# An order planned in the source for the second stage of an S4 and SwiGLU kernel, with the first kernel block's spectra kept in DRAM

## The chip, the cores and the metric

The kernel runs on one core of one Trainium2 chip. The metric is device time in microseconds from the start to the end of one execution; "before" is a median of three runs. A core has a matrix engine (TensorE, PE in the profile), two engines for elementwise work (VectorE, DVE, and ScalarE, ACT), a general engine (GpSimd, POOL) and a queue for transfers (SyncE, SP). Each engine works through its own instructions in the order in which the program lists them, and waits on semaphores for the others.

## What is computed

Two layers, each an S4 long convolution with a residual and then a SwiGLU feed-forward with a residual, over 2048 tokens of width 512 (F = 1376):

```python
def _A_ref(u, ...):                       # L = 2048, D = 512, N = 128
    P = jnp.exp(logdA[:, :, None] * l[None, None, :])
    K = jnp.einsum("dn,dnl,dn->dl", Cc, P, dB).real
    Kf, Uf = rfft(pad(K)), rfft(pad(u))   # length 2 L
    return irfft(Uf * Kf)[:L] + u * Dskip

def _B_ref(x, w_gate, w_up, w_down):
    return (silu(x @ w_gate) * (x @ w_up)) @ w_down

x = A_u
x = x + _A_ref(_layernorm(x), ...)
x = x + _B_ref(_layernorm(x), ...)
x = x + _A_ref(_layernorm(x), ...)
x = x + _B_ref(_layernorm(x), ...)
```

## The kernel before

The sequence is cut into four blocks of 512 tokens. The convolution is done by blocks in the frequency domain: a block's input has a spectrum u (eight pieces of 256 KB: two halves h of the width, four residues q), the convolution kernel has four blocks of spectra w, and output block b is the sum over k = 0..b of w[k] times u[b - k].

The first stage (to about 325 us) makes the kernel's spectra and the first two input spectra; its order is written out by hand in `tc.manual_schedule`, which fixes the order of ScalarE, VectorE and TensorE. Spectra of kernel blocks 1 to 3 go to DRAM (`wdr`); those of block 0 stay in SBUF in `w0r` (16 KB in each partition).

The second stage goes through the eight pairs of layer and block in the order of `SEQ`: (0,0), (0,1), (0,2), (1,0), (0,3), (1,1), (1,2), (1,3). The text calls them blocks 0 to 7 in this order. For each there are:

- `inputs` and `forward` (lines 245 to 279, 680 to 707), from block 2 on: load, layernorm on ScalarE, folding on VectorE (tiles bt and z), 12 matmuls into `pf`, copy to u, and a store to `udr` by a POOL queue for later blocks.
- `ssm` (from line 709): for each of the eight pieces b + 1 complex products, each one multiplication of VectorE over 128x1024 (line 755) and, from the second on, one addition (line 758); joining (759, 760), splitting into two halves of 16 bits (763 on ScalarE, line 232 on VectorE), 12 matmuls into `pi` (774), combining, and per half h two groups of six and eight operations that add to the residual in `xs` (lines 788 to 808).
- `ffn_norm` (line 812), per half s of 256 tokens: layernorm and four transposing transfers issued by SP (line 840).
- `ffn` (line 870), per half s: a `remainder` of 96 columns (lines 852 to 854, its result transposed by four transfers), five groups of 48 matmuls into `pgu` (lines 885 to 887; the tag has two PSUM buffers, which `py` and the remainder share), each evacuated by silu (890, ScalarE), product (891, VectorE), high half (892, ScalarE), low half (893, VectorE); then the down product `py` in two rows r of 128 tokens, 33 matmuls each (lines 899 to 901), each followed by an addition of VectorE (line 904) and a store.

The weights come as 32-bit values and are split into two 16-bit halves each, `his` on ScalarE and `los` on VectorE (lines 641, 646, 667, 670), in 19 parts. The first few are done in the hand-written stage, and so are the rest, after the first norm: one high and one low part in turn, with a `fetch` now and then, behind the last outputs of block 0.

From there the order is the framework's. It schedules all engines by the program's order as priority, with raised priority for evacuations, norms, pi and pf (`tc.high_priority`), and a timeline model of its own. The program lists the convolution of block i + 1 ahead of the feed-forward of block i:

```python
    for i, lb in enumerate(SEQ):
        if i + 1 < len(SEQ):
            take(itertools.chain(*ssm(*SEQ[i + 1])), 100)
        ffn(*lb, ready if i == 0 else None)
```

Of the kernel before, what the change touches and what calls it, by code (L numbers as in the profile page):

```python
# [22 lines left out]
P = 128  # L23
# [18 lines left out]
HALF = 2  # L42
INV = 1
# [38 lines left out]
def kernel(ctx, tc, x, a_re, a_im, b_re, b_im, c_re, c_im, log_dt, d_skip,  # L82
# [10 lines left out]
                xf=1, nn=1, hh=1, hl=1, sg=2, hf=1, stats=2, stats2=2, ef=1)  # L93
# [38 lines left out]
    w0r = sb.tile([P, 2, 4, 2, HD], F32, name="w0r")  # L132
# [106 lines left out]

    def norm_x(n):  # L240
        rs, nb = row_stats(n, 4, 1.0, "stats", lambda r: tl([P, D], "junk", "t1", BF16))
        for c in range(4):
            A.activation(n[:, c], n[:, c], AF.Identity, scale=rs[:, c:c + 1], bias=nb[:, c:c + 1])

    def forward(n, h, eh):


        hs = slice(h * HD, (h + 1) * HD)
        x0, x1, x2, x3 = (n[:, c, hs] for c in range(4))
        bt = tl([P, 7, HD], "bt", "bt")  # L250
        a_, b_, p_, q_, r_, s_, hx = (bt[:, i] for i in range(7))
        stt(a_, x2, HH, x0, OP.add)
        stt(b_, x2, -HH, x0, OP.add)
        A.activation(hx, x2, AF.Copy, scale=HH)
        stt(p_, x3, TT, x1, OP.add)
        stt(r_, x3, -TT, x1, OP.add)
        stt(q_, x1, TT, x3, OP.subtract)
        stt(s_, x1, TT, x3, OP.add)
        for i, q in enumerate(QORD):
            z = z2[:, 0 if eh else i % 2]  # L260
            u_, v_ = ((p_, a_) if q in (0, 3) else (q_, b_))
            stt(z[:, 0], u_, CC if q < 2 else -CC, v_, OP.add)
            stt(z[:, 1], s_ if q in (0, 3) else r_, CC, hx, OP.add if q < 2 else OP.subtract)
            if eh:
                hl = z2[:, 1].bitcast(F16).rearrange("p i (l d) -> p l i d", l=2)
                A.activation(hl[:, 0], z, AF.Copy, scale=256.0)
                stt(hl[:, 1], z, 256.0, hl[:, 0], OP.subtract)
            pf = psml([P, 2, HD], "pf")
            with tc.high_priority(offset=BOOST):
                for o in range(2):  # L270
                    if eh:
                        terms = [(eh[:, q, o + i, le], hl[:, lz, i]) for i in range(2) for le, lz in ((0, 0), (0, 1), (1, 0))]
                    else:
                        terms = [(ef[:, q, o + i], z[:, i]) for i in range(2)]
                    for k, (e, m) in enumerate(terms):
                        PE.matmul(pf[:, o], lhsT=e, rhs=m, start=k == 0, stop=k == len(terms) - 1)  # L276
                u = tl([P, 2, HD], "u", "u")
                A.activation(u, pf, AF.Copy, scale=2.0 ** -16 if eh else 1.0)  # L278
            yield q, u
# [400 lines left out]
    def inputs():  # L680

        for layer, b in SEQ:
# [160 lines left out]
    def remainder(pgu, nh, nlo, hh, hl):  # L843

        rows = TB // P
        fs = slice(F - FR, F)
        pr = pgu.rearrange("p a b t -> p (a b t)")[:, :rows * 2 * FR].rearrange("p (r w f) -> p r w f", r=rows, w=2)
        for r in range(rows):
            rc = slice(r * P, (r + 1) * P)
            for wi in range(2):  # L850
                for k in range(4):
                    PE.matmul(pr[:, r, wi], lhsT=nh[:, k, rc], rhs=wgu(wi, k, 0)[:, fs], start=k == 0, stop=False)
                    PE.matmul(pr[:, r, wi], lhsT=nh[:, k, rc], rhs=wgu(wi, k, 1)[:, fs], start=False, stop=False)
                    PE.matmul(pr[:, r, wi], lhsT=nlo[:, k, rc], rhs=wgu(wi, k, 0)[:, fs], start=False, stop=k == 3)
# [337 lines left out]
```

## Time and profile before

| | |
|---|---|
| median of three runs | 1191.55 us (1190.38 to 1193.35) |
| the profiled execution | 1191.82 us, its span 1190.0 us |
| TensorE busy | 1108.1 us, 93% |
| VectorE busy | 1026.7 us, 86% |
| ScalarE busy | 618.8 us, 52% |
| GpSimd busy | 178.9 us, 15% |
| moved by DMA | 146.91 MB, mean 123 GB/s |
| first feed-forward product (line 885) | at 329.3 us |

The page gives busy times, the span in slices, the chain of work that ended last, the costliest groups of instructions and the transfers. In a row of the order of time the columns are start, duration, engine, line, operation, output and inputs, and in brackets the idle time of the engine ahead of it and what ended it. The duration of a matmul is its whole way through the array; the next one starts before it ends, so the distance of two starts is what one costs.

### The profile page before, as it was taken

The page shows a single profiled execution, that of the slowest core. Times are in us where ns is not written, and L with a number is a line of the kernel's source. Part 1 is how long each engine was busy: PE and PEld are TensorE (multiplying, and loading weights), DVE is VectorE, ACT ScalarE, POOL GpSimd, SP SyncE. Part 2 cuts the span into 40 slices and gives each one's busy share as a digit, 9 for nine tenths or more (in the row PEclk, how much of TensorE's full clock was granted, in tenths as well). Part 3 has the DMA queues.
Part 4 walks back from the last instruction along what each step waited for, and adds up shares of the span by engine and source line. Part 5 has one row for each costly group of instructions (what it writes and reads, how often), then busy time and mean ns, then how long its engine had stood idle before and what let it go on. Part 6 is the DMA issues. An engine that isn't in the chain of part 4 may idle for free.

```text
span 1190.0 us, 25245 instructions
## 1 busy us (share of the span) xinstructions
PE 1108.1 (93%) x10268; PEld 859.4 (72%) x10268; DVE 1026.7 (86%) x1623; ACT 618.8 (52%) x1168; POOL 178.9 (15%) x233
## 2 busy tenths in 40 slices
PE   2979999889978998999999999999999999999998
PEld 2857766667866766777777686868677686877875
DVE  8989999996899989999999999998997899983211
ACT  6998788763255445357744263564533552334211
POOL 3105444432300011011010000210200010000000
PEclk9999999999979998999999999999999999999999
DMA  6454455568468326442334443432445144312000
GB/s 235 124 138 129 109 128 125 118 184 232 146 199 248 103 72 187 129 129 89 103 94 142 135 149 128 145 107 98 130 131 191 45 120 129 114 51 45 14 24 18
DMA packets 138471, 146.91 MB, mean 123 GB/s; under 512 B 77873, under 2 KB 87089, under 8 KB 138354
## 3 DMA queue, kind: packets, MB, share of 16 engines
q1 hardware_dynamic: 133490, 128.51, 35.7%
q0 software_dynamic: 4864, 16.78, 5.8%
q8 instruction: 80, 1.31, 0.5%
q14 instruction: 37, 0.30, 0.1%
HBM read 98.19 MB, written 28.31 MB: 106 GB/s over the span
## 4 chain that ended last, share of the span: by engine, by line
PE 48%; DVE 32%; ACT 9%; issue 6%; DMA 3%; POOL 1%; SPq 1%; DVEq 0%; ACTq 0%; POOLq 0%
PE pgu L885 8%; PE pgu L887 8%; PE pgu L886 8%; PE pi L774 4%; DVE t L755 4%; PE pw L552 3%; PE py L899 3%; PE py L900 3%; PE py L901 3%; PE pf L276 3%; DVE yk L758 2%; DVE z L232 2%; DVE yk L755 2%; DVE im L394 1%; DVE sg L891 1%
## 5 line engine op out<-in xcount | busy, mean ns | idle before, releaser
L885 PE MATMUL pgu<-mix,wsl 128*128 128x256 f16 x1280 | 352.2, 275 | 9.1 <-DVE sg L891 5.5
L886 PE MATMUL pgu<-mix,wsl 128*128 128x256 f16 x1280 | 352.1, 275 | 1.2 <-DVE mix L831 1.2
L887 PE MATMUL pgu<-mix,wsl 128*128 128x256 f16 x1280 | 351.9, 275 | 0.4 <-DVE wsl L646 0.4
L886 PEld LDWEIGHTS <-wsl 128*128 128x128 f16 x1280 | 126.1, 99 | 27.1 <-issue 10.5
L887 PEld LDWEIGHTS <-wsl 128*128 128x128 f16 x1280 | 126.1, 99 | 21.1 <-DVE wsl L646 3.6
L885 PEld LDWEIGHTS <-wsl 128*128 128x128 f16 x1280 | 126.1, 99 | 16.9
L899 PE MATMUL py<-wsl,hh 128*128 128x512 f16 (+1 forms) x352 | 133.6, 380 | 4.3 <-DVE xf L904 2.5
L901 PE MATMUL py<-wsl,hl 128*128 128x512 f16 (+1 forms) x352 | 133.5, 379 | 0.0
L900 PE MATMUL py<-wsl,hh 128*128 128x512 f16 x320 | 121.4, 379 | 0.0
L755 DVE TENSOR_TENSOR t<-uu,w 128x1024 f32<-128x1024 f32 x96 | 117.1, 1220 | 0.7 <-DMA uu<-udr 0.6
L758 DVE TENSOR_TENSOR yk<-yk,t 128x1024 f32<-128x1024 f32 x96 | 117.0, 1219 | 0.3
L890 ACT ACTIVATE sg<-pgu,sc 128x512 f32<-128x512 f32 x80 | 54.5, 682 | 104.2 <-PE pgu L887 97.6
L774 PE MATMUL pi<-yl,mix 128*128 128x256 f16 x672 | 92.3, 273 | 7.5 <-ACT yl L763 6.0
L552 PE MATMUL pw<-kt,ek 128*128 128x256 f32 (+2 forms) x420 | 98.5, 373 | 0.0
L891 DVE SCALAR_TENSOR_TENSOR sg<-pgu,sc,sg 128x512 f32<-128x512 f32 x80 | 59.7, 747 | 43.7 <-ACT sg L890 43.5
L892 ACT ACTIVATE hh<-sg 128x512 f16<-128x512 f32 x80 | 50.1, 626 | 76.6 <-DVE sg L891 76.5
L552 PEld LDWEIGHTS pw<-kt,ek 128*128 128x128 f32 x420 | 78.2, 195 | 9.7
L227 POOL TENSOR_TENSOR rs<-mv,mhalf 128x2 f32<-128x2 f32 (+1 forms) x21 | 39.3, 1870 | 255.1 <-ACT mv L226 240.6
L774 PEld LDWEIGHTS <-mix 128*128 128x128 f16 x672 | 65.3, 98 | 13.6 <-issue 1.8
L276 PE MATMUL pf<-z,eh 128*128 128x256 f16 x576 | 74.9, 275 | 0.0
L763 ACT ACTIVATE yl<-mix,sy 128x512 f16<-128x512 f32 x56 | 40.1, 717 | 63.4 <-DVE mix L760 63.3
L755 DVE TENSOR_TENSOR yk<-u,w0r 128x1024 f32<-128x1024 f32 x56 | 68.3, 1220 | 0.3 <-ACT u L278 0.3
(250 smaller groups left out, 2232.6 us busy)
## 6 DMA issues: line engine op xcount, KB each, us to landing
w<-wdr SPq DMA_DIRECT2D x96, 256.0 KB, 2.7
uu<-udr SPq DMA_DIRECT2D x96, 256.0 KB, 3.0
udr<-u POOLq DMA_DIRECT2D x32, 256.0 KB, 2.4
wdr<-wo SPq DMA_DIRECT2D x96, 64.0 KB, 2.3
udr<-u SPq DMA_DIRECT2D x16, 256.0 KB, 2.5
g<-tmp POOLq DMA_DIRECT2D x8, 512.0 KB, 4.7
g<-btl POOLq DMA_DIRECT2D x8, 512.0 KB, 6.1
n<-xdr SPq DMA_DIRECT2D x4, 1024.0 KB, 5.7
```

The source lines that it names most:

```text
L276: PE.matmul(pf[:, o], lhsT=e, rhs=m, start=k == 0, stop=k == len(terms) - 1)
L552: PE.matmul(pw[:, i], lhsT=e, rhs=kt[:, :, c + 4 * k0:4 * k1:4, :].rearrange("p g k d -> p k g d"), start=c == 0, stop=c == 3)
L755: V.tensor_tensor(t, uu.unsqueeze(1).to_broadcast([P, 2, 2, HD]), w.unsqueeze(2).to_broadcast([P, 2, 2, HD]), OP.mult)
L758: V.tensor_tensor(yk, yk, t, OP.add)
L774: PE.matmul(pi[:, o], lhsT=e, rhs=m, start=k == 0, stop=k == len(terms) - 1)
L885: PE.matmul(o, lhsT=wgu(wi, k, 0)[:, fs], rhs=nh[:, k], start=k == 0, stop=False)
L886: PE.matmul(o, lhsT=wgu(wi, k, 0)[:, fs], rhs=nlo[:, k], start=False, stop=False)
L887: PE.matmul(o, lhsT=wgu(wi, k, 1)[:, fs], rhs=nh[:, k], start=False, stop=k == 3)
L891: V.scalar_tensor_tensor(sg, pgu[:, 1], sc6[:, 4:5], sg, OP.mult, OP.mult)
L899: PE.matmul(py[:, r], lhsT=hh[:n, f, rc], rhs=wd(f, 0)[:n], start=f == 0, stop=False)
L900: PE.matmul(py[:, r], lhsT=hh[:n, f, rc], rhs=wd(f, 1)[:n], start=False, stop=False)
L901: PE.matmul(py[:, r], lhsT=hl[:n, f, rc], rhs=wd(f, 0)[:n], start=False, stop=f == FT - 1)
```

## The change

From the first feed-forward product on, the order of TensorE, VectorE, ScalarE and of the emission to SP and POOL is planned in the source. The program first builds a list of jobs (`plan_splits`, `plan_ssm`, `plan_forward`, `plan_norm`, `plan_ffn`), each with its engine, an estimated duration and latency, the jobs that it depends on, a priority, and buffers that it takes and gives back. `emit` then simulates the engines: it always takes the job that can start first, and among those that can start at the same time on an engine the one with the lowest priority tuple. The instructions are emitted in that order, inside `manual_schedule`.

- Priorities (lower first): evacuations (0, 0, ..), weight splits (0, 1, k), the last outputs of block 0 (0, 2), then the work of block i by (1, i, ..). On TensorE pi and pf have (0, i, ..) and count as ready 1500 ns after their inputs (`MARGIN`).
- The spectra of kernel block 0 are written from `w0r` to `wdr[0]` (2 MB) once, and loaded from there from block 2 on, 256 KB for each of eight pieces of six blocks. The place of `w0r` becomes four more buffers for products and sums (`home`).
- The remainder, pf and the two pi have PSUM tiles of their own (`prs`, `pfs`, `pis`).
- The sums are additions of VectorE (the branch for accumulating transfers is `if k and False`).
- The remaining weight splits, the last outputs of block 0 and the loads of `eih` and `eh` become jobs too. What stands ahead of the first feed-forward product is unchanged but for these.

```diff
+HOP = 150
+SLACK = 0.0
+LAND = 2000
+BUSY = dict(DVE=3300.0, ACT=1500.0)
+MARGIN = 1500.0
+CAP = dict(w=3, uu=3, u=2, big=2, sg=2, pi=2, yl=2, bb=2, dd=2)
...
-    w0r = sb.tile([P, 2, 4, 2, HD], F32, name="w0r")
+    w0r = tl([P, 2, 4, 2, HD], "w0r", "w0")
...
+        def earliest(j):
+            t = free.get(j["eng"], 0.0)
+            for d in j["deps"]:
+                if d["end"] is None:
+                    return None
+                t = max(t, d["end"] + (MARGIN if j["eng"] == "PE" and j["pr"][0] == 0 else 0))
+            for k, n in j["get"]:
...
+                    t = max(t, gave[k][m]["end"])
+            return t
+
+        while any(left.values()):
+            best = None
+            for todo in left.values():
+                ready = [(earliest(j), j["pr"], n) for n, j in enumerate(todo[:400])]
+                ready = [r for r in ready if r[0] is not None]
+                if ready:
+                    t0 = min(r[0] for r in ready)
+                    t0, p, n = min((r for r in ready if r[0] <= t0 + SLACK), key=lambda r: (r[1], r[0], r[2]))
+                    if best is None or t0 < best[0]:
+                        best = t0, todo, n
+            t, todo, n = best
+            j = todo.pop(n)
+            j["fn"]()
+            free[j["eng"]] = t + j["ns"]
+            j["end"] = t + j["lat"]
...
+    def dve(n, ps=False):
+        return n / 0.96 + (128 if ps else 68)
...
+        def turn(r, k):
+            nc.sync.dma_start_transpose(nhl[k][:, :, r * P:(r + 1) * P], nt[:, k])
...
+            a = job("SP", 100, lambda r=r: turn(r, 0), [j], (0, i), [f"nh{s}"] if r == 0 else (), lat=2600)
...
             for r in range(rows):
+                for fl in ((0, 1), (2, 3), (4, 5), (6, 7), (8, 9, 10)):
+                    dep = [d for f in fl for d in ready[f // 2 * 2]] + [split.get(8 + f) for f in fl]
+                    prev = job("PE", len(fl) * 3 * 217, lambda f=mmd, r=r, fl=fl: f(r, fl), dep + [prev], (1, i, s, 9),
+                               ["big"] if r == 0 and fl[0] == 0 else (), ["hh"] if r == rows - 1 and fl[0] == 8 else (),
+                               len(fl) * 3 * 217 + 180)
...
+                j = job("DVE", dve(D, True), addx, [prev], (0, 0, i, s, 9), (), ["big"] if r == rows - 1 else ())
...
-        k = 0
-        while los:
-            split(1, 1) if his else split(0, 1)
...
-    for i, lb in enumerate(SEQ):
-        if i + 1 < len(SEQ):
-            take(itertools.chain(*ssm(*SEQ[i + 1])), 100)
-        ffn(*lb, ready if i == 0 else None)
...
+        eihj = dma(768, lambda: nc.sync.dma_start(eih, c_eih), pr=(1,))
+        split_jobs = plan_splits()
+        outp[0, 1] = [job('DVE', 8 * dve(HD) + 900, lambda f=f: take(f, 1), pr=(0, 2)) for f in rest_outs]
+        evict = [dma(1024, lambda h=h: nc.sync.dma_start(wdr[0, h].rearrange("q p i d -> p q i d"), w0r[:, h]),
+                     pr=(2,)) for h in range(2)]
...
+        for i in range(len(SEQ)):
+            if i + 1 == HALF:
+                ehj = dma(768, load_eh, pr=(2, 2), get=["ef"])
+            if i + 1 < len(SEQ):
+                plan_ssm(i + 1, ehj)
+            normed = [[] if i + s == 0 else plan_norm(i, s) for s in range(T // TB)]
+            plan_ffn(i, normed, split_jobs if i == 0 else {})
+        emit()
```

555 lines of the change are left out of this document (447 added, 108 removed).

## The prediction

> **What bounds the kernel now.** I read the page first, then the stages from the first feed-forward product on, then single waits. From there on TensorE and VectorE are both nearly full, so the question is what the gaps on TensorE are and which of them another order closes.
>
> ```profile
> span 1190.0 us, 25245 instructions
> 329.30:400.00 70.70, 60.96 (x482) 45.01 (x482) 69.49 (x104) 34.89 (x53) 2.22 (x3) 0.88 0.65 202
> 400.00:470.00 70.00, 62.82 (x517) 48.84 (x516) 62.94 (x114) 38.36 (x78) 7.40 (x8) 0.95 0.39 120
> 470.00:760.00 290.00, 287.81 (x2455) 226.36 (x2453) 281.98 (x477) 143.79 (x282) 23.62 (x30) 1.00 0.40 124
> 760.00:1050.00 290.00, 282.49 (x2398) 218.21 (x2396) 268.81 (x432) 128.99 (x247) 25.19 (x25) 1.00 0.40 118
> 1050.00:1186.00 136.00, 135.15 (x1070) 98.90 (x1067) 44.52 (x72) 35.06 (x64) 2.05 (x4) 1.00 0.09 25
> ```
>
> These are the page's span and the table by stage (PE, weight loads, DVE, ACT, POOL busy, then the granted clock, DMA share and GB/s). The reader is to see that TensorE is busy 99% after 470 us, and that two short stages lose time and clock: 329 to 400 and 400 to 470.
>
> Busy time overlaps itself, so I count TensorE's work by instructions times pitch. Counts come from the groups by line, pitches from the order of time and the chain:
>
> ```profile
> L885 PE MATMUL pgu<-mix,wsl 128*128 128x256 f16 x1280 | 352.2, 275 | 9.1 <-DVE sg L891 5.5 <-DVE sgr L861 1.4 <-DMA wdr<-wo 1.1
> L901 PE MATMUL py<-wsl,hl 128*128 128x512 f16 (+1 forms) x352 | 133.5, 379 | 0.0
> L774 PE MATMUL pi<-yl,mix 128*128 128x256 f16 x672 | 92.3, 273 | 7.5 <-ACT yl L763 6.0 <-DVE yl L232 1.5
> L276 PE MATMUL pf<-z,eh 128*128 128x256 f16 x576 | 74.9, 275 | 0.0
> L852 PE MATMUL pgu<-wsl,mix 128*128 128x96 f16 x256 | 37.8, 209 | 3.2 <-DMA mix<-nn 2.7 <-DVE sg L891 0.5
> 1101.89 0.27 PE L885 MATMUL pgu<-mix,wsl 128*128 128x256 f16 x1
> 1111.28 0.27 PE L887 MATMUL pgu<-mix,wsl 128*128 128x256 f16 x1
> 672.60 0.21 PE L852 MATMUL pgu<-wsl,mix 128*128 128x96 f16 x1
> 673.71 0.21 PE L854 MATMUL pgu<-wsl,mix 128*128 128x96 f16 x1
> 1173.38 0.38 PE L900 MATMUL py<-wsl,hh 128*128 128x512 f16 x1
> 1177.27 0.38 PE L900 MATMUL py<-wx,hh 96*128 96x512 f16 x1
> 684.16 1.20 PE pi L774 x11
> 1185.62 0.38 PE L901 MATMUL py<-wsl,hl 96*128 96x512 f16 x1
> ```
>
> The first pair is 86 steps apart: 9.39 / 86 = 0.1092 us. The second pair is 26 steps: 0.0427. The third 18 steps: 0.216. The transform products (pi, pf) take 1.20 / 11 = 0.109. By the first row's 1280 for each of three lines, 885 to 887 make 3840 x 0.1092 = 419.3 us, the remainders (852 to 854) 768 x 0.0427 = 32.8, the down products (899 to 901) 3 x 352 x 0.216 = 228.1, pi and pf 1248 x 0.109 = 136.0. Sum: **816.2 us**, of which a block's feed-forward has (419.3 + 32.8 + 228.1) / 8 = 85.0 and its eight pi 10.5. From 329.3 that would put the last matmul at 1145.5; it starts at 1185.6. So **40.1 us** are lost. By stage: the **ramp** (329 to 400) has 70.70 - 60.96 = 9.7 idle and, at a granted clock of 0.88, 8.5 of slow clock: 18.2. The **gate** of the second block (400 to 470) has 7.2 and 3.5: 10.7. **Later** it is 2.2 + 7.5 + 0.9 = 10.6, and 0.6 hides in the tails of matmuls. After the last matmul come 4.4 us. No order of the same instructions can win more than about 37 of these 40 us, since the first products start at half clock in any case (below).
>
> **The change, part by part.** "All sums on VectorE" changes nothing here: line 758 already adds on VectorE, and the branch for DMA sums is switched off by its condition. No instruction of TensorE, VectorE or ScalarE is added; what changes is their order, and some buffers.
>
> *The ramp.* What stood in TensorE's way:
>
> ```profile
> 351.40 0.11 PEld L887 LDWEIGHTS <-wsl 128*128 128x128 f16 x1 [3.62 <-DVE wsl L646]
> 366.99 1.41 DVE L670 SCALAR_TENSOR_TENSOR wsl<-st,sc,wsl 128x512 f16<-128x512 f32 x2
> 370.45 0.37 PE L885 MATMUL pgu<-mix,wsl 128*128 128x256 f16 x1 [4.30 <-DVE sg L891]
> 330.00:340.00 10.00, 9.10 (x61) 7.21 (x61) 9.43 (x13) 8.88 (x8) 0.00 (x0) 0.70 0.76 263
> ```
>
> VectorE did outputs and block 1's products before the low halves of the weights for which TensorE stood (first row), and later low halves (second row) before the evacuation that frees a PSUM buffer (third row). In the plan evacuations rank first, then the splits, then block 1, and the remainder has a PSUM bank of its own. I take these two stalls and their slow clock as gone. What stays is the start at clock 0.70 (10 x 0.30 = 3.0 us) and 3 us of waits for the last weights: 6 instead of 18.2. The bounds are 3 and 16: near the old value if the 2 MB of spectra that are now written out first push the w_down loads back, since the DMA engines are already 76% busy there. The last outputs of block 0 (two calls of eight operations on VectorE) and, on SP's queue, the loads of eih and eh move behind the first fetches: eih (768 KB behind two fetches of 688 KB, 2.2 MB at 263 GB/s, 8 us) is there by 338, while block 1 comes behind splits on VectorE, and eh is not read before block 2. Both are inside the 3 us; without that cover the first pi holds TensorE up by what eih is late.
>
> The clock itself: the row says 0.70 after the pause ahead of 329. The Trainium skill ("TensorE: Matmul & The Clock Gate", Part 1) puts a halved clock behind an idle window of about 3.4 us and lifts it after as much work; by it, the 4.30 us stall paid again and a wait of 1 us pays nothing. The trace agrees with both: 0.88 in the mean of the ramp, 1.00 in every stage after 470, where the waits are short.
>
> *The gate of block 1.* The feed-forward of block 1 starts when VectorE has finished that block's convolution and a norm with transposes has run:
>
> ```profile
> 330.80:450.50 119.70, 108.54 (x851) 80.98 (x850) 112.25 (x187) 60.52 (x108) 8.18 (x9) 0.94 0.46 145
> 330.80:450.50 119.70, 25.39 (x21) 0.94 0.46 145
> 330.80:450.50 119.70, 13.37 (x11) 0.94 0.46 145
> 330.80:450.50 119.70, 4.74 (x36) 6.59 (x14) 2.47 (x4) 0.94 0.46 145
> 330.80:450.50 119.70, 7.99 (x22) 0.81 (x2) 0.94 0.46 145
> 442.81 0.42 DVE L232 SCALAR_TENSOR_TENSOR xg<-t,xg 128x256 f32<-128x256 f32 x1
> 450.14 0.42 DVE L232 SCALAR_TENSOR_TENSOR xg<-t,xg 128x256 f32<-128x256 f32 x1
> 452.36 0.26 PE L852 MATMUL pgu<-wsl,mix 128*128 128x96 f16 x1 [2.72 <-DMA mix<-nn]
> 454.86 0.26 PE L854 MATMUL pgu<-wsl,mix 128*128 128x96 f16 x1 [2.16 <-DMA mix<-nn]
> ```
>
> The first five rows are one stretch, for all instructions, then for line 755, line 758, the tile z and the tile bt (DVE is the third figure of the first row, the second of the fourth, the first of the others). VectorE was idle 119.70 - 112.25 = 7.5 us and did work of block 2 ahead of the end of block 1: z and bt 10.8 (7.99 holds ten of z's instructions, some 3.8, once more), 6 of the 21 multiplies (block 1 has 16, one of them done earlier) 7.3, and 3 of the 11 adds 3.6. That is 21.7. The plan ranks the lower block first, so I move 21.7 behind and 7.5 away: 450.5 - 29.2 = 421.3, plus 1.2 for the multiply that the old order had done before. The half that the norm of the first rows needs ends 8 operations earlier, 2.7: 419.8. From there to the first product the trace has 452.36 - 443.2 = 9.1, to the second half 11.7: 429 to 431.5. TensorE has 85.0 + 10.5 + 3.0 to do from 329.3 and is done at 427.8. So the gate costs 2 at the least; VectorE will not be free of idle time, and I take **8** with its slow clock, between 2 and 15.
>
> *The wait that the plan does not know.* The two row halves of py lie in one tile. In before the second half never starts until VectorE's add has read the first:
>
> ```profile
> 671.62 0.38 PE L901 MATMUL py<-wsl,hl 96*128 96x512 f16 x1
> 674.34 0.74 DVE L904 SCALAR_TENSOR_TENSOR xf<-py,sc,xf 128x512 f32<-128x512 f32 x1
> 675.13 0.38 PE L899 MATMUL py<-wsl,hh 128*128 128x512 f16 x1 [1.21 <-DVE xf L904]
> 1177.90 0.75 DVE L904 SCALAR_TENSOR_TENSOR xg<-py,sc,xg 128x512 f32<-128x512 f32 x1 [4.21 <-PE py L901]
> 1178.71 0.38 PE L899 MATMUL py<-wsl,hh 128*128 128x512 f16 x1 [0.84 <-DVE xg L904]
>   PE py L899: 4.3, 6
> ```
>
> The old order put other products between (the second half follows at once only in the 6 cases of the last row, 4.3 us, with 0.16 hidden in each 5.3). The plan's job for the second half depends on the matmuls before it alone and ranks right behind the first half, so TensorE stands there with everything queued behind it. At the end of the kernel, with VectorE free, the wait cost 1178.71 - 1177.27 - 2 x 0.216 = 1.0 us, at 675 1.21 + 0.16 = 1.4. There are 16 such places; the only work that the plan puts ahead is a pi or pf that became ready in the last chunk (9 x 0.216 = 1.9 us long; one such product comes every 106 / 16 = 6.6 us), some 30%. So 11 x 1.2 = 13, of which I take 1 as lying in the ramp: **12** (6 to 36; the upper end is 11 times 3.3, the whole way from 671.62 to 675.13 less one pitch).
>
> *What else waits later.* Of 10.6 us, 5.3 were the py waits. The rest are transform products and evacuations a little late. The plan holds pi and pf back by 1.5 us, which covers some: I take **5** (2 to 12).
>
> *Spectra in DRAM.* 48 loads of 256 KB more (12.6 MB) and 2 MB written, over some 650 us: 22 GB/s on top of 120.
>
> ```profile
> w<-wdr SPq DMA_DIRECT2D x96, 256.0 KB, 2.7
> 363.21 1.24 SPq L840 DMA_TRANSPOSE mix<-nn  x1
> ```
>
> A load lands in 2.7 us; with three buffers it is issued three multiplies ahead, with at least two adds between, over 5 x 1.2 = 6 us. It can stand behind four transposes of 1.24 us on SP's queue, which the plan counts at 0.1: 2.7 + 5.0 = 7.7, so now and then a multiply is late by some 2 us. VectorE has that slack after 470 (269 of 290 busy), hence nothing; without that cover, 14 such bursts of 2 us are 28. The freed SBUF gives more buffers for sums that one engine does in order: no gain.
>
> **Sum.** 3.0 + 3 + 8 + 12 + 5 = 31 lost instead of 40.1. Span: 1145.5 + 31 + 4.4 = 1180.9; around the span lie 1191.82 - 1190.0 = 1.8, so **1183 us**. The profiled run is 0.3 above the median of 1191.55.
>
> **The rivals.** (1) *The plan holds*: the py waits are filled or do not appear, the gate costs 2 to 6. 31 - 12 - 4 = 15 lost: 1167. Against it stands that all the py rows above show the wait. The Trainium skill ("PSUM — Partial Sum Buffer", PSUM bank collisions) asks to keep TensorE and VectorE apart only on the same bank, and two rows of 2 KB are two banks; by it the wait could go, but the trace shows it set by the program. (2) *The gaps come back*: VectorE stays busy in the ramp with the same total, DMA holds the weights, and 18.2 + 10.7 shrink by 6 only, which the py waits (12 against 5.3) eat: 40.1 - 6 + 6.7 = 41 lost, 1193. (3) *Slower*: the order is fixed on both sides, so while TensorE stands at py, VectorE, ahead of it, stands at the next evacuation, and the add is queued behind other long operations. Without py I lose 19; the change loses from the point where 11 waits cost (40.1 - 19) / 11 = 1.9 us each. At 3.3, the way at 675, 19 + 36 = 55: 1207. For it: that row. Against it: the add ranks first on VectorE, and past the ramp one operation of VectorE lasts 1.2 at most (25.39 / 21). (4) *The change does not do what it says*, in that loads lead the order: 2 MB in front of w_down, about 8 us at 263 GB/s, in the ramp, and three bursts of late spectra, 6 us: 45 lost, 1197.
>
> **How the numbers follow.** Forecast (1172 to 1188) 0.45; rival 1 0.12; rival 2 0.20; rival 3 0.14; rival 4 0.09. The first two are faster by over 0.3% (about what a measurement of this kernel can tell from no change): 0.57. Rival 2 is within: 0.20. The last two are slower: 0.23. The range is 1166 to 1201: it takes in the times of rivals 1, 2 and 4 and the lower part of rival 3, and leaves out that one's upper end and all unknown costs at their worst at once.
>
> **What would show it.** TensorE idle before the second half of py, ended by VectorE's add, some 11 times at 1.0 to 1.4 us; VectorE's splits done by about 345 and no 4 us stall in the ramp; block 1's feed-forward starting at 430 to 437 instead of 452; clock 1.00 after that; no multiply waiting for w. I am wrong if VectorE idles for DMA in the ramp, if the gate stays at 450, or if the py waits exceed 1.9 us.

## The result and the profile after

The changed kernel takes 1232.88 us (median of 6 runs, 1224.85 to 1237.64) against 1193.53 us (6 runs, 1190.38 to 1195.56) for the kernel before on the same chip: a ratio of 1.033, 95% interval 1.029 to 1.037. The forecast was 1183, with 1201 as the upper end of the range. The profiled execution took 1231.68 us.

First the page of the changed kernel: span, busy times, the loads of the spectra (count, size, median us from issue to landing).

```profile
span 1229.9 us, 25319 instructions
PE 1117.1 (91%) x10268; PEld 860.3 (70%) x10268; DVE 1042.1 (85%) x1623; ACT 615.5 (50%) x1168; POOL 167.7 (14%) x233
w<-wdr SPq DMA_DIRECT2D x144, 256.0 KB, 3.1
```

VectorE is busy 15 us longer than before and TensorE 9, while the span is 40 longer: mostly time in which they stand, not work. The table by stage (columns as in the prediction; its bounds are set against the first feed-forward product, here at 324.75) shows where TensorE stands:

```profile
324.75:395.45 70.70, 60.33 (x493) 45.75 (x493) 62.23 (x92) 43.43 (x74) 3.21 (x4) 0.91 0.66 186
395.45:475.00 79.55, 66.00 (x539) 50.62 (x538) 73.91 (x125) 31.22 (x59) 4.16 (x6) 0.96 0.48 140
475.00:760.00 285.00, 272.75 (x2287) 210.76 (x2286) 260.33 (x429) 130.47 (x256) 16.80 (x26) 0.99 0.45 133
760.00:1050.00 290.00, 269.58 (x2250) 206.56 (x2249) 263.34 (x428) 127.93 (x253) 18.38 (x28) 0.98 0.47 136
1050.00:1226.00 176.00, 170.88 (x1351) 126.50 (x1348) 84.14 (x128) 44.53 (x81) 2.00 (x5) 1.00 0.16 47
```

Idle time plus slow clock, counted as in the prediction:

| us lost by TensorE | before | forecast | after |
|---|---|---|---|
| ramp | 18.2 | 6 | 10.4 + 6.4 = 16.8 |
| gate of block 1 | 10.7 | 8 | 13.6 + 3.2 = 16.8 |
| later | 10.6 | 17 | 37.8 + 8.7 = 46.5 |
| all, from span, first product and 816.2 | 40.1 | 31 | 1229.9 - 4.4 - 324.75 - 816.2 = 84.6 |

The 4.5 us between the rows and the last line are not accounted for: a wait hides 0.16 us in the tail of a matmul, and the clock has two digits, of which half a step is 2.9 us over the 575 us of the third and fourth row. The loss is not in the ramp and the gate, where the change was expected to act, but in the long stage after them. What TensorE waits for there (us in total, times, longest) is in the view of its waits, from 324 us on:

```profile
PE pgu L1262 <- DVE sg L1277: 28.9, 15, 6.3
PE pr L1219 <- DMA mix<-nn: 6.3, 2, 6.1
PE py L1298 <- DVE xg L1310: 4.4, 5, 1.2
PE pgu L1262 <- DVE xf L1310: 3.1, 4, 1.2
PE pgu L1262 <- DVE xg L1310: 2.9, 3, 1.2
PE py L1298 <- DVE xf L1310: 2.0, 2, 1.4
```

The first row was 5.5 us in 3 times: a group of products waits for the evacuation (silu, product) that frees its PSUM buffer. (Line 1277 is the old 891, 1310 the old 904, 1219 the old 854, 1048 the old 755; 1155 and 1180 are ScalarE's part of the norm, 922 that of a block's load, 1175 and 1241 the transposes of norm and remainder.) The waits at py, which the forecast feared, are 6.4 us. ScalarE and VectorE, which do the evacuations, wait for transfers (rows picked from both engines' waits); the last two rows are ScalarE's waits for transposes in the kernel before (line 223 is the norm's, like 1155; 837 the old 1180):

```profile
ACT nn L1155 <- DMA mix<-nn: 15.3, 5, 6.0
ACT nn L1180 <- DMA mix<-nn: 9.4, 5, 5.6
ACT junk L922 <- DMA n<-xdr: 7.7, 2, 7.1
DVE nn L1182 <- DMA mix<-nn: 8.6, 5, 3.1
DVE yt L1048 <- DMA w<-wdr: 6.4, 4, 3.4
DVE t L1048 <- DMA w<-wdr: 5.1, 2, 3.2
ACT nn L837 <- DMA mix<-nn: 7.8, 7, 2.2
ACT nn L223 <- DMA mix<-nn: 7.6, 5, 2.5
```

The waits for transposes are 24.7 us instead of 15.4, and the longest 6.0 instead of 2.5.

The order of time shows how one becomes the other. The rows are of several engines and the SP queue (SPq):

```profile
375.94 0.26 PE L1219 MATMUL pr<-wsl,mix 128*128 128x96 f16 x1 [6.13 <-DMA mix<-nn]
...
431.59 0.42 DVE L239 SCALAR_TENSOR_TENSOR xg<-t,xg 128x256 f32<-128x256 f32 x1
435.50 0.42 DVE L239 SCALAR_TENSOR_TENSOR xg<-t,xg 128x256 f32<-128x256 f32 x1
446.98 0.21 PE L1217 MATMUL pr<-wsl,mix 128*128 128x96 f16 x1
...
456.95 3.90 SPq L1241 DMA_TRANSPOSE hh<-sgr  x2
460.97 2.44 SPq L1241 DMA_TRANSPOSE hl<-sgr  x2
463.47 0.57 SPq L1028 DMA_DIRECT2D w<-wdr  x1
464.14 1.23 SPq L1175 DMA_TRANSPOSE mix<-nn  x1
466.39 1.22 DVE L1048 TENSOR_TENSOR t<-uu,w 128x1024 f32<-128x1024 f32 x1 [3.22 <-DMA w<-wdr]
467.02 0.63 ACT L1180 ACTIVATE nn<-nn 128x512 f16<-128x512 f32 x1 [5.58 <-DMA mix<-nn]
467.56 0.67 ACT L1274 ACTIVATE sg<-pgu,sc 128x512 f32<-128x512 f32 x1
469.83 0.69 DVE L1182 TENSOR_TENSOR nn<-nn 128x512 f16<-128x512 f32 x1 [1.55 <-DMA mix<-nn]
470.44 0.74 DVE L1277 SCALAR_TENSOR_TENSOR sg<-pgu,sc,sg 128x512 f32<-128x512 f32 x1
471.24 0.37 PE L1262 MATMUL pgu<-mix,wsl 128*128 128x256 f16 x1 [6.30 <-DVE sg L1277]
```

Four transposes of a remainder hold SP until 463.4. The load of w is issued at 463.47, and VectorE stands for it at line 1048. ScalarE stands 5.58 us at line 1180 for a buffer that transposes still read. The silu at 467.56 is behind it in ScalarE's line, the product at 470.44 behind another late transpose in VectorE's, and TensorE has been waiting for both: 6.30 us. Ahead of TensorE's stalls at 654, 953 and 1006 lies such a wait too (VectorE 3.43 us for w at 650, ScalarE 7.06 for a block's load at 948 and 5.97 for transposes at 1000); the one at 771 has only 2.27 us of VectorE for w at 760 ahead of it, and what makes it is not shown.

**The plan's own clock.** `emit` gives each job a start and an end. By that arithmetic the last end of this kernel lies 868.1 us after the first feed-forward product. The kernel before needed 1190.0 - 329.3 = 860.7 for the same work. So the plan itself is 7.4 us longer than what the old order took, and the chip then took 1229.9 - 324.75 = 905.2, a **slip** of 37.1 us behind the plan. Both numbers are used below: the slip of a kernel is its span less the first product's time less its plan's end. The first product comes anywhere between 324.75 and 330.8 in the profiles below, though they share what stands ahead of it, so its 4.5 us here are no gain. First product, span and slip come from the one profiled execution, which lies up to 5 us from the median (x5: 1234.49 against 1229.54), so differences of slip below some 5 us say little.

### The profile page after: what moved, and what is told of

The parts are those of the page before. It is cut to its first block, busy times and chain, and to the rows that moved or that the text cites. A ratio compares the mean times of both kernels' runs of the same rounds, so it can differ in the third digit from the quotient of the medians.

```text
span 1229.9 us, 25319 instructions
## 1 busy us (share of the span) xinstructions
PE 1117.1 (91%) x10268; PEld 860.3 (70%) x10268; DVE 1042.1 (85%) x1623; ACT 615.5 (50%) x1168; POOL 167.7 (14%) x233
## 4 chain that ended last, share of the span: by engine, by line
DVE 43%; PE 29%; ACT 12%; DMA 7%; issue 7%; SPq 2%; POOL 1%; DVEq 0%; POOLq 0%; ACTq 0%
DVE yt L1048 5%; PE pgu L1262 4%; PE pgu L1263 4%; PE pgu L1264 4%; DVE yt L1055 3%; DMA mix<-nn 3%; PE py L1298 3%; DVE sg L1277 3%; PE py L1300 3%; PE py L1299 3%; DVE z L239 3%; PE pw L518 2%; DVE yk L1055 2%; DVE t L1048 2%; DVE t L239 2%
## 5 line engine op out<-in xcount | busy, mean ns | idle before, releaser
L1262 PE MATMUL pgu<-mix,wsl 128*128 128x256 f16 x1280 | 353.9, 276 | 36.6 <-DVE sg L1277 28.9
L1084 PE MATMUL pi<-yl,mix 128*128 128x256 f16 x672 | 85.0, 277 | 3.0 <-DVE yl L239 2.8
L1073 ACT ACTIVATE yl<-mix,sy 128x512 f16<-128x512 f32 x56 | 40.1, 716 | 84.5 <-DVE mix L1070 84.1
L1048 DVE TENSOR_TENSOR yt<-uu,w 128x1024 f32<-128x1024 f32 x58 | 70.5, 1220 | 6.4 <-DMA w<-wdr 6.4
L984 PE MATMUL pf<-z,eh 128*128 128x256 f16 x576 | 71.0, 273 | 2.8 <-DVE z L239 2.6
L1300 PEld LDWEIGHTS <-hl 128*128 128x128 f16 (+1 forms) x352 | 34.3, 97 | 46.2 <-issue 4.2
L984 PEld LDWEIGHTS <-eh 128*128 128x128 f16 x576 | 56.2, 98 | 13.0 <-issue 3.4
L1299 PEld LDWEIGHTS <-hh 128*128 128x128 f16 (+1 forms) x352 | 34.4, 98 | 42.3 <-issue 12.4
```

Of the source, the lines that this page charges most:

```text
L984: PE.matmul(pfs[:, o_], lhsT=e, rhs=z, start=k == 0, stop=k == len(terms) - 1)
L1048: V.tensor_tensor(t, u.unsqueeze(1).to_broadcast([P, 2, 2, HD]), w.unsqueeze(2).to_broadcast([P, 2, 2, HD]), OP.mult)
L1084: PE.matmul(pis[n % 2][:, o_], lhsT=e, rhs=m, start=k == 0, stop=k == len(terms) - 1)
L1262: PE.matmul(d, lhsT=wgu(wi, k, 0)[:, fs], rhs=nh[:, k], start=k == 0, stop=False)
L1299: PE.matmul(o["py"][:, r], lhsT=hhl["h"][:n, f, rc], rhs=wd(f, 1)[:n], start=False, stop=False)
L1300: PE.matmul(o["py"][:, r], lhsT=hhl["l"][:n, f, rc], rhs=wd(f, 0)[:n], start=False, stop=f == FT - 1)
```

## The experiments

Theory A: transfers come later than the plan counts, stop ScalarE or VectorE in line, and the evacuations behind them are late. B: the 48 extra loads of block 0's spectra are what crowds the transfers. C: the wait of py's second half, which the plan does not know, is where the slip starts. A1 and A2 part A in two, D and E come later. x7, x9 and x10 have no slip in this sense and stand below. Line numbers move by one where a line was added. All times are medians, with 95% intervals of the ratio to before.

| kernel | plan's end | time | ratio | first product, span | slip |
|---|---|---|---|---|---|
| after | 868.1 | 1232.88 | 1.029 to 1.037 | 324.75, 1229.9 | 37.1 |
| x1 SP in plan order | 868.1 | 1238.28 | 1.036 to 1.042 | 325.98, 1240.4 | 46.3 |
| x2 transposes' figures | 872.8 | 1210.09 | 1.012 to 1.018 | 325.81, 1205.5 | 6.9 |
| x3 spectra resident | 865.1 | 1225.78 | 1.026 to 1.031 | 326.18, 1221.4 | 30.1 |
| x4 py wait in plan | 877.7 | 1238.23 | 1.035 to 1.042 | 329.42, 1235.2 | 28.1 |
| x5 transposes, SP's time only | 879.7 | 1229.54 | 1.024 to 1.033 | 330.44, 1232.7 | 22.6 |
| x6 transposes, landing only | 875.7 | 1223.92 | 1.020 to 1.028 | 326.82, 1221.7 | 19.2 |
| x8 mended plan (four edits) | 862.6 | 1195.27 | 0.998 to 1.002 | 328.81, 1193.8 | 2.4 |
| x11 transposes, resident | 863.0 | 1199.42 | 1.003 to 1.007 | 330.81, 1200.5 | 6.7 |
| x12 mended but transposes | 863.4 | 1202.84 | 1.005 to 1.010 | 328.20, 1199.4 | 7.8 |
| x13 ScalarE's cost | 868.0 | 1217.37 | 1.017 to 1.023 | 327.91, 1215.2 | 19.3 |
| x14 remainder second | 862.6 | 1220.19 | 1.018 to 1.024 | 328.24, 1218.6 | 27.8 |
| x15 ScalarE's cost, resident | 867.2 | 1209.03 | 1.010 to 1.016 | 328.44, 1207.2 | 11.6 |
| x16 remainder second, resident | 865.2 | 1221.12 | 1.019 to 1.025 | 329.39, 1222.2 | 27.6 |
| x17 transposes, ScalarE's cost | 870.8 | 1199.18 | 1.002 to 1.007 | 325.97, 1196.8 | 0.0 |

**x1: SP's queue in the plan's order.** In after, only TensorE, VectorE and ScalarE are fixed; the framework orders SP.

```diff
-        emit()
+        with tc.manual_schedule(engines={mybir.EngineType.SP}):
+            emit()
```

> Edit: SP's transfers of the planned stage are issued in the plan's order as well (the changed kernel fixes only the order of the three compute engines; SP's is chosen by the framework). Theory A: the changed kernel runs 37 us behind its own plan because loads and transposes come later than the plan counts, and a late one stops ScalarE or VectorE, with the PSUM evacuations behind it. If the order on SP's queue is what makes them late, the big stalls of TensorE ahead of line 1262 (28.9 us ended by VectorE's line 1277) fall to under 15 and the time to 1205 to 1218. Theory B (the additional loads of block 0's spectra make everything late) and theory C (the py wait that the plan does not know) expect no change: 1227 to 1238.

No gain, rather 5 us lost, which the intervals do not part: that the framework orders SP is not what makes transfers late.

**x2: larger figures for the transposes**, 1.25 us of SP's time, as the rows show, and 3.65 us to landing.

```diff
+TURN, TURNED = 1250, 3650
-            a = job("SP", 100, lambda r=r: turn(r, 0), [j], (0, i), [f"nh{s}"] if r == 0 else (), lat=2600)
+            a = job("SP", TURN, lambda r=r: turn(r, 0), [j], (0, i), [f"nh{s}"] if r == 0 else (), lat=TURNED)
...
```

(and so in the other two places)

> Edit: the plan counts a transposing transfer with 1250 ns of SP's queue and 3650 ns until it has landed, instead of 100 and 2600. The plan's own end moves from 868.1 to 872.8 us after the first feed-forward product. Theory A, in the form that the plan's figure for these transfers is the cause: the orders of ScalarE and VectorE no longer stand behind unfinished transposes, TensorE's wait for them at the second half of block 0 (6.1 us at 375.9) shrinks, and the slip of 37 us falls by 10 to 20: 1215 to 1228. Theories B and C: the slip stays and the time follows the plan: 1233 to 1240.

22.8 us faster, though the plan's end is 4.7 later: the slip falls from 37.1 to 6.9. Rows from its waits of TensorE and of ScalarE:

```profile
PE pi L1085 <- ACT yl L1074: 10.6, 2, 8.4
...
PE pgu L1263 <- DVE sg L1278: 7.6, 11, 1.6
ACT nn L1156 <- DMA mix<-nn: 1.6, 1, 1.6
ACT nn L1181 <- DMA mix<-nn: 0.9, 1, 0.9
```

The waits for evacuations are down from 28.9 to 7.6, the longest from 6.3 to 1.6, ScalarE's two waits for transposes from 24.7 to 2.5. Theory A holds here.

**x3: block 0's spectra stay in SBUF**, so the 2 MB are not written and the 48 loads not made; products and sums have one buffer each again.

```diff
-                if k or i > 1:
+                if k:
...
-        yseq, tseq = itertools.cycle(("y", "s0", "s1")), itertools.cycle(("t", "s2", "s3"))
+        yseq, tseq = itertools.cycle(("y",)), itertools.cycle(("t",))
...
-        evict = [dma(1024, lambda h=h: nc.sync.dma_start(wdr[0, h].rearrange("q p i d -> p q i d"), w0r[:, h]),
-                     pr=(2,)) for h in range(2)]
```

> Edit: block 0's spectra stay in SBUF; the 2 MB written and 48 loads of 256 KB go away, and sums use one product and one sum buffer as in the kernel before. Theory B: the additional loads are what is late: 15 us or more come back, 1205 to 1218, and waits of VectorE for w (11.5 us) fall to under 2. Theory A: only a part, since transposes and the other loads stay: 1222 to 1231. Theory C: 1228 to 1238.

7 us faster, at the edge of the noise (the two intervals overlap); in the profile, 3.0 by the plan's end and 7.0 by the slip. B is at most a part, not the cause.

**x4: the plan knows the wait of py's second half.**

```diff
-f=mmd, r=r, fl=fl: f(r, fl), dep + [prev], (1, i, s, 9),
+f=mmd, r=r, fl=fl: f(r, fl), dep + [prev, added], (1, i, s, 9),
...
-                j = job("DVE", dve(D, True), addx, [prev], (0, 0, i, s, 9), (), ["big"] if r == rows - 1 else ())
+                j = added = job("DVE", dve(D, True), addx, [prev], (0, 0, i, s, 9), (), ["big"] if r == rows - 1 else ())
```

> Edit: the plan's job for the second half of py also depends on VectorE's addition for the first half, so the plan puts other work there. The plan's own end moves from 868.1 to 877.8. Theory C: the py waits (6.4 us at line 1298, and behind them those of 1262 on the additions, 6.0) are the slip's cause; the order now holds and the time is that of the plan plus little: 1205 to 1220. Theories A and B: the waits vanish as waits but the plan has the same gaps, so the time stays at 1228 to 1242.

No gain. The slip falls by 9 and the plan's end rises by 9.6. C is not the cause.

**x5 and x6: which figure of the transposes?** A1 says SP's time, A2 the landing.

```diff
+TURN, TURNED = 1250, 2600   # x5
+TURN, TURNED = 100, 3650    # x6
```

> After with a transposing transfer counted at 1250 ns of SP's time in the plan instead of 100; its landing stays at 2600 ns. The plan itself now ends 879.7 us after the first feed-forward product (4 worse than with the landing alone, 11.6 worse than in after), so 1204.5 would be the time if it were kept. Theory A1 (what is missing in the plan is SP's occupancy: four transposes hold the queue for 5 us and the loads behind them come late): most of the 37 us of slip goes, 1207 to 1218 us. Theory A2 (what is missing is the landing: the plan lets the waiting engines come 1 us too early, again and again): the slip stays at 25 or more, 1230 or above.

> After with the landing of a transposing transfer counted at 3650 ns in the plan instead of 2600; it still takes 100 ns of SP's time. The plan ends 875.7 us after the first feed-forward product, 1200.4 if it were kept. Theory A1 (SP's occupancy): the loads behind transposes stay late, slip 25 or more, 1225 to 1238 us. Theory A2 (landing): 1205 to 1215.

Neither wins. By slip each takes about half (22.6 and 19.2 left of 37.1; 6.9 with both), and each alone makes a plan that ends later than with both. In time x5 is not told from after (1.024 to 1.033 against 1.029 to 1.037). A transpose holds SP 1.2 us (row at 464.14 above) where the plan has 0.1: that figure was wrong. From issue to landing it takes, in the median of the transfers' view of after,

```profile
mix<-nn SPq DMA_TRANSPOSE x60, 3.1
```

where the plan has 2.6; single ones take 2.3 to 9.3, and those of the remainder 2.4 in the median. So 3.65 is not the measured time but one with a margin, and x5, whose figures are nearer to the medians, brought no clear gain. The step from 2.6 to 3.65 is worth 9 us of time alone and 19 beside 1.25 (x2 against x5); how much of that is the margin stays open, since no run has 3.1.

**x7: block 0's spectra in DRAM in the kernel before**, in the framework's order.

```diff
-                    if k == 0:
+                    if k == 0 and SEQ.index((layer, b)) < HALF:
                         w, uu = w0r[:, h, q], u
                     else:
                         w = tl([P, 2, HD], "w", "w")
                         nc.sync.dma_start(w, wdr[k, h, q])
...
+    for h in range(2):
+        nc.sync.dma_start(wdr[0, h].rearrange("q p i d -> p q i d"), w0r[:, h])
     for i, lb in enumerate(SEQ):
```

> Before, in the framework's own order, with the spectra of kernel block 0 written to DRAM (2 MB) and loaded from there from block 2 on: 48 loads of 256 KB more; the freed SBUF is not used. Theory A (only a fixed order turns a late load into a stall): TensorE has slack against VectorE here and the order was made with the loads known, so within 5 us of before, 1190 to 1198. Theory B (the extra loads cost in themselves, as the 7 us won by leaving them out of after suggest): 1198 or above.

1193.98 us, ratio 0.997 to 1.001: nothing. The loads land nearly as fast as they did (2.7 before; page of x7), and VectorE waits 0.4 us for them, where it waits 11.5 in after:

```profile
w<-wdr SPq DMA_DIRECT2D x144, 256.0 KB, 2.8
```

So the extra traffic is free in an order that was made with it, and costs at most some 7 us in one that is late already.

**x8: the plan mended in four places**: transposes as in x2, spectra as in x3, and

```diff
-        return n * 0.833 + (161 if acc else 68)
+        return n * 0.833 + (375 if acc else 170)
...
-            order = (0, 2, 4, 6, FT - 1, 8) if i == 0 and s == 0 else (FT - 1, 0, 2, 4, 6, 8)
+            order = (0, 2, 4, 6, FT - 1, 8) if i == 0 and s == 0 else (0, FT - 1, 2, 4, 6, 8)
```

> After with four edits of the plan: transposes at 1250 ns of SP and 3650 ns to landing, ScalarE's operations at the mean fixed cost of the trace (170 ns, with sums 375, instead of 68 and 161), spectra of block 0 kept in SBUF, and the remainder after the first group of a half instead of ahead of it. The plan ends 862.6 us after the first feed-forward product, 10.1 earlier than with the transposes' costs alone. Theory A (the time is the plan's own end plus a slip of some 8 us that is left): 324.8 + 862.6 + 8 = 1195, between 1190 and 1200, about the time of before and not clearly below it. Rival (slip is a property of a fixed order on SP-fed engines and stays whatever the plan counts): 1205 or above, as with the transposes' costs alone.

1195.27 us, the time of before (0.998 to 1.002): the whole loss is back. Its largest wait of TensorE, and then two stages of it:

```profile
PE pgu L1263 <- DVE sg L1278: 7.3, 10, 2.0
```

```profile
328.80:399.50 70.70, 64.33 (x532) 48.28 (x532) 66.50 (x97) 44.22 (x74) 7.11 (x4) 0.93 0.64 198
399.50:480.00 80.50, 71.05 (x558) 54.17 (x557) 78.40 (x135) 38.86 (x80) 5.04 (x9) 0.92 0.49 133
```

Here the ramp loses 6.4 + 4.9 = 11.3 (before 18.2), the gate 9.5 + 6.4 = 15.9 (before 10.7). Of what the plan wins in the one it gives back most in the other, where VectorE is busy 78.4 of 80.5 us.

**x9 and x10: the same lists as a priority only.** `emit()` stands outside `manual_schedule`, so that the framework orders all engines; x9 has the plan of after, x10 the mended one.

```diff
-        emit()
+    emit()
```

> After with the planned list emitted outside manual_schedule: the same jobs in the same order, but as a priority only; the framework orders all engines with its own timeline model, as in before. Nothing of the plan's figures is changed. Theory A (the plan's figures are wrong and the fixed order turns each late transfer into a stall of an engine with all that is behind it): the framework moves other work ahead of what is late, 1190 to 1210 us. Rival (the sequence itself is bad, however it is enforced): 1225 or above.

> The mended plan (transposes and ScalarE at their measured cost, spectra of block 0 kept in SBUF, remainder after the first group) emitted outside manual_schedule, as a priority only. Theory A (the order is right as soon as the costs are; fixing it is worth little or nothing): within 8 us of the mended plan in fixed order, 1187 to 1203 us. Rival (a framework order that starts from any other list is worse than both): 1205 or above.

1215.25 (1.013 to 1.022) and 1215.44 us (1.015 to 1.025). The framework makes the same time of both lists, x9 between its two expectations. A fixed order is 18 us worse than that with the plan's first figures and 20 better with the mended ones, so fixing the order is no loss by itself; the forecast of 1187 to 1203 for x10 was wrong. Where the framework's order loses is seen in x9:

```profile
PE pt L792 <- ACT nn L790: 8.7, 1, 8.7
335.92 1.44 ACT L607 ACTIVATE wsl<-st,sc 128x1376 f16<-128x1376 f32 x1 [5.91 <-DMA st<-in_B_w_up_dram]
341.86 0.37 PE L1262 MATMUL pgu<-mix,wsl 128*128 128x256 f16 x1 [1.77 <-ACT mix L795]
```

ScalarE has a weight split ahead of the first norm and stands for its load, and TensorE stands 8.7 us for that norm (2.0 in before). The first feed-forward product comes at 341.86 (342.27 in x10). From there to the end it is 1207.9 - 341.86 = 866.0 us (867.7 in x10), about the 865.0 of x8 and 39 less than after. That is not all the order's doing, since some 27 us of VectorE's work of the stage are done ahead of that product (717 us of it are left, 745 in after); but the first list with its wrong figures does not make 905 us of this stage when the framework orders it.

**x11 and x12: the mended plan taken apart.** x11 has the edits of x2 and x3 alone, x12 all of x8 but the transposes (written here against x8).

```diff
-TURN, TURNED = 1250, 3650   # x12, against x8
+TURN, TURNED = 100, 2600
```

> After with the transposes at 1250 ns of SP and 3650 ns to landing, and the spectra of block 0 kept in SBUF; ScalarE's costs and the place of the remainder as in after. The plan ends 863.0 us after the first feed-forward product (872.8 without the second edit, 862.6 with all four). Theory A (the time is the plan's end plus a small slip): 324.8 + 863.0 + 8 to 13 = 1196 to 1201 us. Rival (ScalarE's true costs are what made the mended plan hold): a slip of 20 or more, 1207 or above.

> The mended plan with the transposes counted again at 100 ns of SP and 2600 ns to landing, as in after; ScalarE's costs, the spectra in SBUF and the remainder's place stay mended. The plan's own end is the same within 0.8 us (863.4 against 862.6 us after the first feed-forward product), so any difference is slip behind the plan. Theory A (the transposes' figures are what the order breaks on): 15 to 30 us above the mended plan's 1195, 1210 to 1225 us, with waits of TensorE for evacuations above 2.1 us back. Rival (with block 0's 48 loads gone and ScalarE's costs right the transposes no longer matter): within 5 us of 1195.

x11 came out as theory A has it. x12 did not: at the same plan's end the transposes are worth 5.4 us of slip and 7.6 of time, not 15 to 30. Something else in the mended plan also cures most of it.

**x13 to x16: ScalarE's cost (D) or the place of the remainder (E)**, each alone and with the spectra resident; the diffs are those of x8 and x3.

> After with ScalarE's operations counted at a fixed cost of 170 ns (375 with sums) instead of 68 (161); nothing else. The plan ends 868.0 us after the first feed-forward product (868.1 in after), so the difference is slip. Theory D (ScalarE is at the head of every stall: counted 72 us short over the stage, it falls behind by itself, and late transposes find no room): slip 15 or less, 1205 to 1215 us. Rival E (the place of the remainder is what matters): slip 30 or more, 1223 to 1238.

> After with the remainder behind the first group of a half instead of ahead of it; nothing else. The plan ends 862.6 us after the first feed-forward product (868.1 in after). Theory D (ScalarE's cost): slip 30 or more, 1218 to 1233 us. Rival E (the remainder ahead of the first group puts its four transposes right behind the norm's four on SP, and with them the loads of the next block): slip 15 or less, 1200 to 1210.

> As with ScalarE's mended cost alone, and the spectra of block 0 kept in SBUF. The plan ends 867.2 us after the first feed-forward product. Theory D: slip 12 or less, 1200 to 1209 us. Rival E: slip near the 30 of the resident spectra alone, 1218 to 1230.

> As with the remainder in second place alone, and the spectra of block 0 kept in SBUF. The plan ends 865.2 us after the first feed-forward product. Theory D: slip near 30, 1216 to 1228 us. Rival E: slip 12 or less, 1198 to 1207.

ScalarE's cost takes the slip from 37.1 to 19.3, from 30.1 to 11.6, and (x16 to x12) from 27.6 to 7.8: 18 to 20 us each time, less than D had for x13 (15 or less left). The place of the remainder takes 9.3, 2.5 and (x15 to x12) 3.8, where E had 18 and more. E falls. What the plan has wrong is seen in the groups of after:

```profile
L1274 ACT ACTIVATE sg<-pgu,sc 128x512 f32<-128x512 f32 x80 | 54.4, 681 | 102.0 <-PE pgu L1264 100.6
L1280 ACT ACTIVATE hh<-sg 128x512 f16<-128x512 f32 x80 | 50.1, 627 | 73.6 <-DVE sg L1277 50.3
```

The plan counts 512 x 0.833 + 68 = 495 ns for each of these. Over the stage it gives ScalarE 298 us of work, and the fourth column of the table by stage adds up to 43.4 + 31.2 + 130.5 + 127.9 + 44.5 = 377.6. The Trainium skill ("ScalarE: Activation LUTs", What ACT_TABLE_LOAD costs) has 186 ns plus 0.833 ns an element for an operation with immediate scale and bias, 93 ns more for an operand by pointer, and 93 ns of overlap back to back: 613 to 706 ns for 512 elements, and about 0.1 us less in a row. The trace agrees within 4% (627 and 681), and the cost function of the plan does not.

**x17: both groups of figures mended, nothing else changed.**

> After with the two mended figures alone: transposes at 1250 ns of SP and 3650 ns to landing, ScalarE's operations at a fixed cost of 170 ns (375 with sums). The spectra of block 0 stay in DRAM and the remainder ahead. The plan ends 870.8 us after the first feed-forward product. If the two miscounts make the slip, it is 2 to 7 us here, 1200 to 1206 us with a first product at 325 to 331 and 1.8 us around the span. If the 48 extra loads make part of it by themselves, it stays above 9, 1207 or above.

1199.18 us, and the slip is 0.0, under what was expected. TensorE's waits:

```profile
PE pi L1085 <- DVE yl L240: 9.7, 4, 4.5
PE py L1299 <- DVE xg L1311: 6.7, 8, 1.6
PE pi L1085 <- ACT yl L1074: 5.3, 1, 5.3
PE pgu L1263 <- DVE sg L1278: 4.8, 9, 1.5
```

With the 48 loads still there and the remainder still ahead, two groups of figures account for the whole slip. That any other order would have done as well does not hold: x1, x3, x4, x14 and x16 change an order too, with these figures left as they were, and keep 27.6 to 46.3 us. (A slip of nothing is not a perfect plan: it counts 820.6 us for TensorE where the products take 816.2, which about covers the cold start.) What is left against before is the plan's own end, 870.8 - 860.7 = 10.1 us.

No version beat the kernel before. The mended plan equals it.

## Why the prediction was wrong, step by step

The second stage became 905.2 - 860.7 = 44.5 us longer: 7.4 by the plan's own end, 37.1 by slip behind it.

- **Spectra in DRAM and what stands on SP's queue: the step that failed.** The prediction saw that a load can stand behind four transposes "which the plan counts at 0.1", got 2 us for it, and went on: "VectorE has that slack after 470 (269 of 290 busy), hence nothing". It holds for an order that the framework makes with the loads in it (x7: nothing for the 48 loads). In a line that was planned with too small figures, a waiting VectorE or ScalarE holds up all that is behind it, evacuations too, and it is TensorE that pays: 28.9 us of waits for evacuations instead of 5.5. The cover was judged by VectorE's share of busy time, when the question was what stands next in its line; and the share is that of 760 to 1050 us, while the prediction's own table has 282 of 290 for the stage ahead of it. With larger figures for the transposes 30.2 of the 37.1 us of slip go (x2). The bound that was given up (14 bursts of 2 us, 28) is near the slip by chance: it was put down to the loads alone, for which x3 has 7 at most, and the transposes' own waits, 15.3 + 9.4 us at ScalarE, were not in it.
- **The plan's costs against the trace: left out.** No step compared the cost of ScalarE in `act` with the durations in the profile of before. It was worth 18 to 20 us of slip (x13, x15, x16 to x12). The two terms overlap: with both mended the slip is 0.0 (x17).
- **The gate.** "I move 21.7 behind and 7.5 away": of these 29.2 us, 10 came. Block 1's last output ends at 435.92, 111.2 us after the first product; in before it was 450.56 - 329.3 = 121.3. VectorE was still idle for 111.17 - 101.98 = 9.2 us ahead of it (first row of the last fence; 4.9 of them at the remainder at 375), and did two multiplies and nine small operations of block 2: a planner that takes the job that can start first fills a hole in its own time with later work, whatever its rank. From the output that the norm of the first rows needs, at 431.59 + 0.42 = 432.01, to the first product it then took 15.0 us instead of 9.1, so block 1's products start 122.2 us after the first product instead of 123.1. The sign given ("if the gate stays at 450") came true.
- **The ramp.** 6 was forecast, 16.8 came. The two old stalls of 3.6 and 4.3 us are gone, as forecast, and VectorE does not idle for the weights. In their place TensorE stands 6.13 us at 375.94 for the transposes of the second norm.
- **The py waits.** 12 forecast, 6.4 in 7 cases, and 6.0 more where a group waits behind the same additions (line 1310). Together that is the size forecast, in part by luck, since the second half of it is another wait, for the PSUM buffer; none is above 1.4 us, and the prediction called itself wrong at 1.9. They were no part of what went wrong (x4).
- **What else waits later.** 5 forecast; with the py waits 17, measured 46.5: this is where the failed step shows.
- **The sum.** It took for granted that an order by those ranks reaches what the ranks aim at. Its own arithmetic, before any surprise, ends 7.4 us later than the order that it replaces, with 43 us of TensorE idle.
- **The rivals.** The third had the right kind of mechanism (the order is fixed on both sides, the evacuations are queued behind something) with the wrong trigger: py instead of late transposes and too small costs. It had 1207. The fourth named the spectra: x3 gives them 7 us at most, where it had 14 (8 in the ramp, 6 in late loads).

The clock followed the stalls (last two rows; the first is the stretch up to block 1's last output):

```profile
324.75:435.92 111.17, 98.15 (x789) 74.74 (x789) 101.98 (x164) 56.80 (x100) 4.38 (x6) 0.94 0.53 154
364.00:384.00 20.00, 12.95 (x102) 9.10 (x101) 13.83 (x20) 7.55 (x17) 0.20 (x1) 0.83 0.91 219
464.00:484.00 20.00, 13.70 (x128) 11.70 (x126) 13.18 (x22) 8.43 (x16) 0.54 (x1) 0.83 0.75 197
```

The last two windows of after hold the stalls of 6.13 and 6.30 us; between 340 and 364 and between 384 and 464, where none is above 2.2 us, it is 1.00. This agrees with the prediction's reading (by the Trainium skill, "TensorE: Matmul & The Clock Gate", Part 1, the clock is halved after an idle window of about 3.4 us). x17 has two waits above that, 5.3 and 4.5 us at pi, both between 440 and 460, where its clock is 0.74; its mean is 0.987 against 0.979.

## What to carry to other kernels

An order that is fixed by a planner is as good as the planner's costs: before anything else, set each cost in it beside the duration in a trace, the queue time of a DMA and the fixed part of short operations above all, leave room above the median of a landing (x2 and x6 against x5 and after speak for it), and run the plan's arithmetic to its end, since its total is a forecast that can be compared with the old stage. That an engine has slack in the mean does not make a late transfer free: ask what stands behind the waiting instruction. And a slip that two corrections each cure is not the sum of them: it took the pair, and each in several settings, to see both.

## What the hardware showed that was not expected

The median landing of a norm's transpose, 60 in each kernel, runs from 2.4 us (before, x3, x16) to 3.2 (x17), and it does not go with the slip: x16 has 2.4 and 27.6 us of slip, x17 has 3.2 and none, and x7 has 2.9 at the time of before. Nor do the bytes alone decide it, since x8 moves what before moves (146.90 MB, 123 GB/s) and has 3.0. And the way from the start to the first feed-forward product, the same instructions but for a few transfers, varied from 324.75 to 330.8 us between the profiles of the table, so that a start 4.5 us earlier says nothing of a change.
